# A fused attention and feed-forward kernel: wider transposes and score matmuls at the opening, two moved steps, one store on another queue

## Chip, cores and metric

The kernel runs on one core of a Trainium2 chip. The metric is the device time of one execution in microseconds (us); a kernel is given as the median of several executions. The engines are TensorE (PE; its weight loads are listed apart as PEld), VectorE (DVE), ScalarE (ACT), GpSimd (POOL) and SyncE (SP). POOL, SP and ACT also issue DMA transfers.

## What is computed

Attention with a local window of 96 positions and 8 global positions, for 4 batches, 8 heads, 768 positions and head size 64, and then a feed-forward layer from 512 to 2048 and back on its 3072 rows:

```
scores = q @ k.T / 8 + bias        # bias = -slope[head] * distance
scores = where(keep, scores, -1e9) # keep: first 8 positions, or the last 96
a = softmax(scores);  x = (a @ v), heads side by side   # 3072 x 512
r = max(x @ w_in, 0)
out = (s * r*r + b) @ w_out        # float32
```

TensorE works on bf16 copies and adds up in float32.

## The kernel before

The 3072 rows are cut into 12 granules of 256 rows (two blocks of 128), three to a batch; granule j has all 8 heads, as four head pairs `hp`. The order of the work on every engine is the order of the program text: it is written out by hand from line 856 on, and no scheduler changes it.

Per granule the steps are these.

- **Loading.** POOL issues the loads of k, q and v (L92, L104, L112), which turn float32 into bf16. All weights (`w_in` in 8 slices at L129, `w_out` in 4 at L135) go through the same POOL queue. Granule 0 alone is loaded raw by SP and ACT (L150) and cast by ACT and DVE (`cast`, L157 and L159) into `nat`, laid out as partition, head, block, element. From granule 5 on a one-element copy on POOL (`pace`, L125) holds the next loads back until some earlier result is there.
- **Transposing q and k**, so that the head's 64 elements lie on partitions (`kT`, `qT`). Granule 0: `T_mm` (L257), 8 transposes on TensorE per call, each of one head and one block (128x64). Granules 1 and 2: `T_quads` (L272), 32 transposes of 64x64 per call; their rows are spread over partitions four at a time. `T_ev` (L293) copies the result from PSUM into `kT` or `qT`, one half (two head pairs) per call, on DVE (L305) or ACT (L307). From granule 3 on SP issues DMA transposes instead (`XBk`, L319, and `XBq`, L327).
- **Scores.** `S_mm` (L406) multiplies a key block by a query block for the two heads of a pair, head 0 on the upper 64 partitions and head 1 on the lower 64. In the first granule of a batch (0, 3, 6, 9) a pair takes 6 matmuls: keys 0 with queries 0, keys 1 with queries 1, keys 0 with queries 1. In the others it takes 8. `SB_mm` (L387) adds the bias on TensorE for granule 0 and one pair of granule 1. `S_post` (L426) takes the exponential on ACT (L431); `S_mul` multiplies by a template of the bias on DVE (L441, L445). `SS` does scores and both for two pairs.
- **Attention output.** `A` (L453, matmuls at L474) and the division on DVE (L491, L492); then a transpose to `xT` on TensorE (L510, L530) or by DMA (L544).
- **First layer.** `P1(j, fp)` (L558): 8 matmuls of 128x256 (L565) for 256 of the 2048 columns, in the two `psh` PSUM buffers in turn; relu on ACT (L581, L583) or DVE; the square on DVE later (`flush` at L556, `Q` at L602).
- **Second layer.** Granules 0 to 2: `P2` (L635). From granule 3 on the product of 2x2 blocks is done with seven block products in place of eight: `W_mm` (L715, matmuls at L741), from sums of weights `W_tw` (L689, DVE, L697), made once, and sums of activations `W_sw` (L704, DVE, L713). `W_post` and `W_add` (L751) finish it, and SP stores it. `W_end` (L800) does this for the last granule with four stores: L820, L823 and twice L838.

PSUM tiles come from five pools by tag: `psh` (two buffers), `pso`, `av`, `scA` and `scB` (one each).

Two places of the hand-written order matter below. The first is at lines 932 to 948, after granule 1's attention: squares of granule 0, then `P1(0, 5)`, `P1(1, 0)` to `P1(1, 3)`, `P1(0, 6)`, and the transposes of granule 2 among the last groups. The second is lines 1077 to 1086:

```
    P1(3, 5)
    W_tw(4, 0, 4)
    P1(3, 6)
    P1(3, 7)
    flush()
    W_sw(3, 3)
    W_tw(4, 4, 8)
```

Of the kernel before, what the change touches and what calls it, by code (L numbers as in the profile page):

```python
# [9 lines left out]
BF16 = mybir.dt.bfloat16  # L10
# [8 lines left out]
def kernel(  # L19
# [13 lines left out]
    nc = tc.nc  # L33
    P = nc.NUM_PARTITIONS

    B, H, S, D = q.shape
# [4 lines left out]
    GB = 2  # L41
    GT = GB * P
# [14 lines left out]
    ldp = ctx.enter_context(tc.tile_pool(name="ldp", bufs=3))  # L57
# [81 lines left out]

    raw32 = gpool.tile([P, 2, H, GB * D], F32, name="raw32", tag="gT")  # L140
    for nm in "kq":
        nat[nm, 0] = ldp.tile([P, H, GB * D], BF16, name=f"{nm}nat", tag=f"{nm}nat")

    def first(nm, half):
        src = (q if nm == "q" else k)[0, 4 * half : 4 * half + 4, 0:GT, :]
# [6 lines left out]

    def cast(nm, half, eng=None):
        hs = slice(4 * half, 4 * half + 4)
        i, o = raw32[:, "kq".index(nm), hs, :], nat[nm, 0][:, hs, :]
        if eng is None:
            nc.vector.tensor_copy(o, i)  # L157
        else:
            nc.scalar.copy(o, i)  # L159
# [95 lines left out]
    tps = {}  # L255

    def T_mm(j, half, nm, tag="psh", own=False):  # L257
        a = 0 if nm == "k" else 1
        if own or (j, half) not in tps:
            tps[j, half] = PS[tag].tile([P, 2, 2, GT], BF16, name="ps_t", tag=tag)  # L260
        ps = tps[j, half]
        tps[j, half, nm] = ps
        for e in range(2):
            for i in range(GB):
                for hi in range(2):
                    nc.tensor.transpose(
                        ps[hi * D : (hi + 1) * D, a, e, i * P : (i + 1) * P],
                        nat[nm, j][:, 4 * half + 2 * e + hi, i * D : (i + 1) * D],
                        ident[:],
                    )  # L270

    def T_quads(j, nm, tags=("psh", "psh"), own=False, both=None):  # L272
        a = 0 if nm == "k" else 1
        if both:
            t = PS[both].tile([P, 2, 2, 2, GT], BF16, name="ps_t2", tag=both)
            for half in range(2):
                tps[j, half] = t[:, half]
        for half in range(2):
            if own or (j, half) not in tps:
                tps[j, half] = PS[tags[half]].tile([P, 2, 2, GT], BF16, name="ps_t", tag=tags[half])  # L280
            tps[j, half, nm] = tps[j, half]
        for e in range(2):
            for i in range(4):
                for half in range(2):
                    r = slice(half * D, (half + 1) * D)
                    for hi in range(2):
                        nc.tensor.transpose(
                            tps[j, half][hi * D : (hi + 1) * D, a, e, i * D : (i + 1) * D],
                            nat[nm, j][r, 2 * e + hi, i * D : (i + 1) * D],
                            ident[r, r],  # L290
                        )

    def T_ev(j, half, nm, eng=None, es=(0, 1)):  # L293
        b, g = bg(j)
        a = 0 if nm == "k" else 1
        if j not in qT:
            qT[j] = qtp.tile([P, HP, GT], BF16, name="qT", tag="qT")
        e0, e1 = es[0], es[-1] + 1
        n = GB if j == 0 else 4
        src = tps[j, half, nm][:, a, e0:e1, :].rearrange("p e (i t) -> p e t i", i=n)  # L300
        hs = slice(2 * half + e0, 2 * half + e1)
        dst = kT[b % 2][:, hs, g * GT : (g + 1) * GT] if nm == "k" else qT[j][:, hs, :]
        dst = dst.rearrange("p e (t i) -> p e t i", i=n)
        if eng is None:
            nc.vector.tensor_copy(dst, src)  # L305
        else:
            nc.scalar.copy(dst, src)  # L307
# [98 lines left out]
    def S_mm(j, hp, biased=False, which=None):  # L406
        b, g = bg(j)
        ps = sps[j, hp] if biased else sc_tile(j, hp, which)
        own = [(kT[b % 2][:, hp, (g * GB + i) * P : (g * GB + i + 1) * P], i) for i in range(GB)]
        if g == 0:  # L410
            plan = [own[0] + (0,), own[1] + (1,), (own[0][0], 1, 2)]
        else:
            ko = kos[j]
            plan = [own[0] + (0,), own[1] + (2,), (ko[:, hp, 0, :], 0, 1), (ko[:, hp, 1, :], 1, 3)]
        for n_, (kt, i, oc) in enumerate(plan):
            for hi in range(2):
                r = slice(hi * D, (hi + 1) * D)
                nc.tensor.matmul(  # L418
                    ps[:, hi, oc * P : (oc + 1) * P],
                    lhsT=kt[r, :],  # L420
                    rhs=qT[j][r, hp, i * P : (i + 1) * P],
                    start=not biased,
                    stop=not biased or n_ == len(plan) - 1,
                )
# [133 lines left out]
    def P1(j, fp, sq="dve", tag="psh", relu="act"):  # L558
        if j not in gT:
            gT[j] = gpool.tile([P, FC, GT], BF16, name="gT", tag="gT")  # L560
        ps = PS[tag].tile([P, 2, GT], F32, name="ps_1", tag=tag)
        for i in range(2):
            fc = 2 * fp + i
            for kc in range(KC):
                nc.tensor.matmul(  # L565
                    ps[:, i, :],
                    lhsT=w_in_bf[:, kc, fc * P : (fc + 1) * P],
                    rhs=xT[j][:, kc, :],
                    start=(kc == 0),
                    stop=(kc == KC - 1),  # L570
                )
# [228 lines left out]
    def W_end(j):  # L800
        o = wt.setdefault((j, "o"), work.tile([P, 2, DM], F32, name="o_pr", tag="o_pr", bufs=3))
        lo, hi = slice(0, HC), slice(HC, DM)
        W_mm(j, 1)
        W_sw(j, 2)
        W_post(j, 1)
        W_mm(j, 5)
        v = W_part(j, "u3")
        W_add(j, v, "b", bvec[:, hi])
        W_sw(j, 4)
        W_mm(j, 6)  # L810
        W_post(j, 6)
        t = W_part(j, "t")
        W_add(j, t, "b", wt[j, "u2"])
        W_mm(j, 2)
        W_post(j, 2)
        W_mm(j, 7)
        W_add(j, o[:, 1, hi], "a", v)
        u4 = W_part(j, "u1")
        W_add(j, u4, "a", bvec[:, lo])
        nc.sync.dma_start(W_rows(j)[:, 1, hi], o[:, 1, hi])  # L820
        W_mm(j, 0)
        W_add(j, o[:, 0, hi], "d", t)
        nc.sync.dma_start(W_rows(j)[:, 0, :], o[:, 0, :])  # L823
        for e in range(2):
            ps = ps_h.tile([P, 2, GT], F32, name="ps_e", tag="psh")[:, 0, 0:P]
            cs = slice(e * P, (e + 1) * P)
            for f in range(HF):
                nc.tensor.matmul(
                    ps,
                    lhsT=g_blk(j, 1, 1)[:, f, :],  # L830
                    rhs=tw[:, 3, f, cs],
                    start=f == 0,
                    stop=f == HF - 1,
                )
            nc.vector.scalar_tensor_tensor(
                out=o[:, 1, cs], in0=ps, scalar=s_bc[:], in1=u4[:, cs], op0=ALU.mult, op1=ALU.add
            )
            nc.sync.dma_start(W_rows(j)[:, 1, cs], o[:, 1, cs])  # L838
# [54 lines left out]
    A(0, 3, "pso")  # L893
    XT_half(0, 0, "act", "av")
    KO_own(0)
    T_quads(1, "q", both="scB")
    T_ev(1, 0, "q", "act")
    SB_mm(1, 0)
    XT_half(0, 1, "dve", "psh")
# [31 lines left out]
    XT_half(1, 1, "dve", "pso")  # L931
    for f in range(5):
        Q(0, f)
    P1(0, 5)
    P1(1, 0)
    P1(1, 1)
    P1(1, 2)
    P1(1, 3)
    P1(0, 6)
    T_quads(2, "k", ("pso", "av"))  # L940
    T_ev(2, 0, "k")
    T_ev(2, 1, "k", "act")
    P1(0, 7)
    T_quads(2, "q", ("pso", "av"))
    T_ev(2, 0, "q")
    T_ev(2, 1, "q", "act")
    make_tmpl(0, 2, 1, 3)
# [130 lines left out]
    Q(3, 2)  # L1078
    P1(3, 4)
    P1(3, 5)  # L1080
    W_tw(4, 0, 4)
    P1(3, 6)
    P1(3, 7)
    flush()
    W_sw(3, 3)
    W_tw(4, 4, 8)

    def P1s(j, fp, n):
# [163 lines left out]
```

## Time and profile before

| what | value |
|---|---|
| median of 5 executions | 208.61 us (208.28 to 210.1) |
| the profiled execution: its own time | 208.28 us |
| its span, first to last instruction | 206.4 us |
| PE busy | 198.6 us (96%) |
| weight loads busy | 160.4 us (78%) |
| DVE busy | 173.6 us (84%) |
| ACT busy | 114.3 us (55%) |
| POOL busy | 77.0 us (37%) |
| granted TensorE clock, mean | 0.999 |
| the chain that ended last | PE 72%, DMA 18%, POOL 6% |

The profile is one execution. Its timeline gives for a group of like instructions the start, the time from the first start to the last end, engine, line, operation, tiles, shape, count, and in brackets the idle time of the engine before it with what ended it. Matmuls are pipelined: a single 128x256 matmul of the first layer is listed with 273 ns, but eight in a row start every 0.109 us. So the price of a block of matmuls is read from its start to the start of the next block, not from the sum of its durations. The chain that ended last is followed back from the last instruction, at each step to what released it; time on that chain is what sets the end. Time of an engine off the chain can grow as long as it stays covered.

### The profile page before, as it was taken

To read this page: it belongs to the slowest core of one execution; us is meant where nothing else is said; L and a number is where in the kernel's file an instruction comes from. 1 tells how busy PE (TensorE), PEld (TensorE's weight loads), DVE (VectorE), ACT (ScalarE), POOL (GpSimd) and SP (SyncE) were. 2 spreads that over 40 slices of the span, in tenths; PEclk is the share of its full clock that TensorE was granted. 3 is DMA by queue.
4 is the path that set the end of the run, shared out by engine and by line. 5 is a ranking of instruction groups with operands and counts; after the bars stand their busy time and mean duration, and the time that the engine had idled before them with its cause. 6 is when DMAs were issued, how large, how long until landed. Compare 5 with 4: busy or idle time off the path is not lost.

```text
span 206.4 us, 5617 instructions
## 1 busy us (share of the span) xinstructions
PE 198.6 (96%) x2288; PEld 160.4 (78%) x2293; DVE 173.6 (84%) x418; ACT 114.3 (55%) x171; POOL 77.0 (37%) x98
## 2 busy tenths in 40 slices
PE   7988899999899999999999999999999999999993
PEld 2657776545765788888988988988988988988883
DVE  5887677699898999988799799788799799787693
ACT  5888588353895676636536536536446546524400
POOL 8994673854646019519029109109000000000000
PEclk9999999999999999999999999999999999999999
DMA  5999999999999988969999939999996041040022
GB/s 165 192 184 197 191 195 190 174 148 152 111 118 184 198 233 90 142 130 112 191 117 127 203 59 118 201 126 97 189 120 174 8 118 37 0 152 5 0 105 102
DMA packets 104858, 27.64 MB, mean 134 GB/s; under 512 B 91520, under 2 KB 102144, under 8 KB 104832
## 3 DMA queue, kind: packets, MB, share of 16 engines
q0 software_dynamic: 70976, 13.11, 91.9%
q1 hardware_dynamic: 32800, 13.64, 33.6%
q10 hardware_dynamic: 1056, 0.52, 0.9%
q8 instruction: 18, 0.29, 0.6%
q14 instruction: 8, 0.07, 0.2%
HBM read 27.26 MB, written 6.29 MB: 163 GB/s over the span
## 4 chain that ended last, share of the span: by engine, by line
PE 72%; DMA 18%; POOL 6%; ACT 1%; issue 1%; DVE 0%; POOLq 0%; ACTq 0%
PE ps L565 34%; PE ps_w L741 15%; PE ps_wb L741 7%; DMA w_in_bf<-in_moe_w_in_dram 5%; DMA qnat<-in_q_dram 5%; DMA w_out_bf<-in_moe_w_out_dram 4%; PE ps_wa L741 4%; PE ps_av L474 4%; PE ps_s L418 4%; DMA qT<-qnat 4%; PE ps L635 3%; POOL w_in_bf L129 2%; POOL vaug L112 2%; ACT gT L583 1%; POOL knat L92 1%
## 5 line engine op out<-in xcount | busy, mean ns | idle before, releaser
L565 PE MATMUL ps<-xT,w_in_bf 128*128 128x256 bf16 x768 | 96.2, 273 | 1.9 <-DMA w_in_bf<-in_moe_w_in_dram 1.8
L565 PEld LDWEIGHTS <-w_in_bf 128*128 128x128 bf16 x768 | 72.6, 98 | 12.4 <-DMA w_in_bf<-in_moe_w_in_dram 2.5
L583 ACT ACTIVATE gT<-ps 128x512 bf16<-128x512 f32 x72 | 43.1, 598 | 58.7 <-PE ps L565 56.5
L431 ACT ACTIVATE pt<-ps_s 128x1024 bf16<-128x1024 f32 (+1 forms) x48 | 43.1, 951 | 6.9 <-PE ps_s L418 4.6
L741 PEld LDWEIGHTS <-sw 128*128 128x128 bf16 x288 | 28.1, 98 | 3.5
L602 DVE TENSOR_TENSOR gT<-gT 128x512 bf16<-128x512 bf16 x74 | 28.1, 415 | 1.7 <-ACT gT L583 1.6
L125 POOL COPY pdum<-xT 1x1 bf16<-1x1 bf16 x5 | 6.7, 1339 | 46.0 <-DMA xT<-xn 46.0
L445 DVE TENSOR_TENSOR pt<-pt,tmpl 128x1024 bf16<-128x1024 bf16 x31 | 20.8, 685 | 2.8 <-ACT pt L431 2.8
L112 POOL DMA_DIRECT2D vaug<-in_v_dram x24 | 21.6, 919 | 4.2 <-DMA w_out_bf<-in_moe_w_out_dram 1.6
L741 PEld LDWEIGHTS <-gT 128*128 128x128 bf16 x208 | 19.7, 98 | 3.2 <-issue 0.2
L492 DVE TENSOR_TENSOR xn<-ps_av,rc 128x256 bf16<-128x256 f32 x48 | 20.4, 424 | 1.7
L635 PE MATMUL ps<-w_out_bf,gT 128*128 128x512 bf16 x76 | 18.7, 380 | 0.2
L741 PE MATMUL ps_w<-tw,sw 128*128 128x256 bf16 x144 | 18.7, 273 | 0.0
L581 ACT ACTIVATE gT<-ps 128x512 bf16<-128x512 f32 x23 | 13.6, 599 | 7.5 <-PE ps L565 7.3
L751 DVE SCALAR_TENSOR_TENSOR u<-ps_w,s_bc,bvec 128x256 f32<-128x256 f32 x27 | 12.9, 478 | 5.7 <-PE ps_w L741 5.7
L474 PEld LDWEIGHTS <-pt 128*128 128x128 bf16 x352 | 15.2, 98 | 3.1 <-DVE pt L445 0.8
L104 POOL DMA_DIRECT2D knat<-in_k_dram x18 | 15.8, 886 | 3.9 <-DMA kT<-knat 2.7
L104 POOL DMA_DIRECT2D qnat<-in_q_dram x18 | 16.0, 901 | 3.5 <-DMA w_out_bf<-in_moe_w_out_dram 2.6
L474 PE MATMUL ps_av<-vaug,pt 128*128 128x65 bf16 x224 | 16.1, 194 | 0.1
L635 PEld LDWEIGHTS <-gT 128*128 128x128 bf16 x96 | 8.7, 97 | 8.9
L418 PE MATMUL ps_s<-qT,kT 64*128 64x128 bf16 x224 | 12.7, 219 | 1.1 <-DMA qT<-qnat 1.0
L491 DVE RECIPROCAL rc<-ps_av 128x4 f32<-128x4 f32 x48 | 8.5, 177 | 5.9 <-PE ps_av L474 5.7
(102 smaller groups left out, 241.5 us busy)
## 6 DMA issues: line engine op xcount, KB each, us to landing
out_dram<-o_pr SPq DMA_DIRECT2D x19, 256.0 KB, 4.5
vaug<-in_v_dram POOLq DMA_DIRECT2D x24, 128.0 KB, 7.6
knat<-in_k_dram POOLq DMA_DIRECT2D x22, 128.0 KB, 6.0
qnat<-in_q_dram POOLq DMA_DIRECT2D x22, 128.0 KB, 7.0
w_in_bf<-in_moe_w_in_dram POOLq DMA_DIRECT2D x8, 256.0 KB, 8.2
w_out_bf<-in_moe_w_out_dram POOLq DMA_DIRECT2D x4, 512.0 KB, 10.0
out_dram<-o_pr SPq DMA_DIRECT2D x2, 512.0 KB, 2.7
raw<-in_q_dram ACTq DMA_DIRECT2D x2, 256.0 KB, 4.8
```

The source lines that it names most:

```text
L104: nc.gpsimd.dma_start(t[:, i, :, :], src[b, :, sb * P : (sb + 1) * P, :].rearrange("h p d -> p h d"))
L112: nc.gpsimd.dma_start(vaug[b % 2][:, sb, :, 0:D], v[b, :, sb * P : (sb + 1) * P, :].rearrange("h p d -> p h d"),)
L418: nc.tensor.matmul(ps[:, hi, oc * P : (oc + 1) * P], lhsT=kt[r, :], rhs=qT[j][r, hp, i * P : (i + 1) * P], start=not biased, stop=not bias ...
L431: nc.scalar.activation(pt[:, :, 0:n], ps[:, :, 0:n], ACT.Exp, scale=QSCALE)
L445: nc.vector.tensor_tensor(x, x, m.unsqueeze(2).to_broadcast((P, 2, GB, 2 * P)), ALU.mult)
L474: nc.tensor.matmul(av[:, i, hi, :], lhsT=pt[:, hi, c * P : (c + 1) * P], rhs=vv, start=n_ == 0, stop=n_ == len(ops) - 1,)
L492: nc.vector.tensor_tensor(xn[j][:, :, 2 * hp : 2 * hp + 2, :], av[:, :, :, 0:D], rc[:].to_broadcast((P, GB, 2, D)), ALU.mult,)
L565: nc.tensor.matmul(ps[:, i, :], lhsT=w_in_bf[:, kc, fc * P : (fc + 1) * P], rhs=xT[j][:, kc, :], start=(kc == 0), stop=(kc == KC - 1),)
L583: nc.scalar.activation(gs.rearrange("p f (r t) -> p f r t", r=2), ps[:].rearrange("p f (t r) -> p f r t", r=2), ACT.Relu,)
L602: nc.vector.tensor_tensor(gs, gs, gs, ALU.mult)
L635: nc.tensor.matmul(po[j, tb], lhsT=gT[j][:, fc, tb * P : (tb + 1) * P], rhs=w_out_bf[:, fc, :], start=(fc == 0), stop=(fc == FC - 1),)
L741: nc.tensor.matmul(wt[j, ps], lhsT=lhs[:, f, :], rhs=rhs[:, f, :], start=first and f == 0, stop=f == HF - 1, skip_group_check=True,)
```

## The change

Six edits:

1. Granule 0's `nat` is laid out as partition, block, head, element, and the casts write into it in that order. `T_mm` then transposes two heads at once: 4 transposes of 128x128 per call in place of 8 of 128x64.
2. `T_quads` takes all 128 partitions at once: 16 transposes of 128x64 per call in place of 32 of 64x64. Both halves of k, or of q, lie in one PSUM tile; before, a half's k and q shared a tile. Granule 1's k uses one `psh` buffer, its q `scB`; granule 2's k uses `pso`, its q `av`.
3. `S_mm` for the first granule of a batch multiplies keys 0 with both query blocks in one matmul of 256 columns, written to two separate column ranges: 4 matmuls per head pair in place of 6.
4. `P1(1, 0)` goes before `P1(0, 5)`.
5. `W_tw(4, 0, 4)` goes from before `P1(3, 6)` to after `W_sw(3, 3)`.
6. In `W_end` the store of rows 0 (L823) is issued by ACT's queue, no longer by SP's.

In all 112 matmuls and as many weight loads fewer are issued: 16 by `T_mm`, 64 by `T_quads`, 32 by `S_mm`.

```diff
-        nat[nm, 0] = ldp.tile([P, H, GB * D], BF16, name=f"{nm}nat", tag=f"{nm}nat")
+        nat[nm, 0] = ldp.tile([P, GB, H, D], BF16, name=f"{nm}nat", tag=f"{nm}nat")
...
-        i, o = raw32[:, "kq".index(nm), hs, :], nat[nm, 0][:, hs, :]
+        i = raw32[:, "kq".index(nm), hs, :].rearrange("p h (i d) -> p h i d", i=GB)
+        o = nat[nm, 0][:, :, hs, :].rearrange("p i h d -> p h i d")
...
-        tps[j, half, nm] = ps
+        tps[j, half, nm] = ps[:, a]
         for e in range(2):
+            h = 4 * half + 2 * e
             for i in range(GB):
+                nc.tensor.transpose(
+                    ps[:, a, e, i * P : (i + 1) * P],
+                    nat[nm, j][:, i, h : h + 2, :],
+                    ident[:],
+                )
+
+    def T_quads(j, nm, tag="psh"):
+        t = PS[tag].tile([P, 2, 2, GT], BF16, name="ps_t", tag=tag)
+        for half in range(2):
+            tps[j, half, nm] = t[:, half]
+        for e in range(2):
+            for i in range(4):
                 for hi in range(2):
                     nc.tensor.transpose(
-                        ps[hi * D : (hi + 1) * D, a, e, i * P : (i + 1) * P],
-                        nat[nm, j][:, 4 * half + 2 * e + hi, i * D : (i + 1) * D],
+                        t[hi * D : (hi + 1) * D, :, e, i * D : (i + 1) * D],
+                        nat[nm, j][:, 2 * e + hi, i * D : (i + 1) * D],
                         ident[:],
                     )
...
-            plan = [own[0] + (0,), own[1] + (1,), (own[0][0], 1, 2)]
+            plan = [(own[0], slice(0, GT), None), (own[1], qs[1], 1)]
...
+                if oc is None:
+                    dst = ps[:, hi].rearrange("p (a c) -> p a c", a=GB)[:, :, 0:P]
+                else:
+                    dst = ps[:, hi, oc * P : (oc + 1) * P]
                 nc.tensor.matmul(
-                    ps[:, hi, oc * P : (oc + 1) * P],
+                    dst,
                     lhsT=kt[r, :],
-                    rhs=qT[j][r, hp, i * P : (i + 1) * P],
+                    rhs=qT[j][r, hp, qc],
...
-        nc.sync.dma_start(W_rows(j)[:, 0, :], o[:, 0, :])
+        nc.scalar.dma_start(W_rows(j)[:, 0, :], o[:, 0, :])
...
-    T_quads(1, "q", both="scB")
+    T_quads(1, "q", "scB")
...
+    P1(1, 0)
     P1(0, 5)
-    P1(1, 0)
...
-    T_quads(2, "k", ("pso", "av"))
+    T_quads(2, "k", "pso")
...
-    T_quads(2, "q", ("pso", "av"))
+    T_quads(2, "q", "av")
...
-    W_tw(4, 0, 4)
     P1(3, 6)
     P1(3, 7)
     flush()
     W_sw(3, 3)
+    W_tw(4, 0, 4)
     W_tw(4, 4, 8)
```

More of the change, by code (lines that the diff above doesn't have):

```diff
@@ L261, in T_mm @@
         ps = tps[j, half]
-        tps[j, half, nm] = ps
+        tps[j, half, nm] = ps[:, a]
         for e in range(2):
+            h = 4 * half + 2 * e
             for i in range(GB):
+                nc.tensor.transpose(
[9 more added lines that the diff above has]
+            for i in range(4):
                 for hi in range(2):
                     nc.tensor.transpose(
-                        ps[hi * D : (hi + 1) * D, a, e, i * P : (i + 1) * P],
-                        nat[nm, j][:, 4 * half + 2 * e + hi, i * D : (i + 1) * D],
+                        t[hi * D : (hi + 1) * D, :, e, i * D : (i + 1) * D],
+                        nat[nm, j][:, 2 * e + hi, i * D : (i + 1) * D],
                         ident[:],
                     )
[L272 to L291, printed above, removed]
     def T_ev(j, half, nm, eng=None, es=(0, 1)):
@@ L299, in T_ev @@
         n = GB if j == 0 else 4
-        src = tps[j, half, nm][:, a, e0:e1, :].rearrange("p e (i t) -> p e t i", i=n)
+        src = tps[j, half, nm][:, e0:e1, :].rearrange("p e (i t) -> p e t i", i=n)
         hs = slice(2 * half + e0, 2 * half + e1)
@@ L408, in S_mm @@
         ps = sps[j, hp] if biased else sc_tile(j, hp, which)
-        own = [(kT[b % 2][:, hp, (g * GB + i) * P : (g * GB + i + 1) * P], i) for i in range(GB)]
+        own = [kT[b % 2][:, hp, (g * GB + i) * P : (g * GB + i + 1) * P] for i in range(GB)]
+        qs = [slice(i * P, (i + 1) * P) for i in range(GB)]
         if g == 0:
-            plan = [own[0] + (0,), own[1] + (1,), (own[0][0], 1, 2)]
+            plan = [(own[0], slice(0, GT), None), (own[1], qs[1], 1)]
         else:
             ko = kos[j]
-            plan = [own[0] + (0,), own[1] + (2,), (ko[:, hp, 0, :], 0, 1), (ko[:, hp, 1, :], 1, 3)]
-        for n_, (kt, i, oc) in enumerate(plan):
+            plan = [(own[0], qs[0], 0), (own[1], qs[1], 2)]
+            plan += [(ko[:, hp, i, :], qs[i], 2 * i + 1) for i in range(GB)]
+        for n_, (kt, qc, oc) in enumerate(plan):
             for hi in range(2):
                 r = slice(hi * D, (hi + 1) * D)
+                if oc is None:
+                    dst = ps[:, hi].rearrange("p (a c) -> p a c", a=GB)[:, :, 0:P]
+                else:
+                    dst = ps[:, hi, oc * P : (oc + 1) * P]
                 nc.tensor.matmul(
-                    ps[:, hi, oc * P : (oc + 1) * P],
+                    dst,
                     lhsT=kt[r, :],
-                    rhs=qT[j][r, hp, i * P : (i + 1) * P],
+                    rhs=qT[j][r, hp, qc],
                     start=not biased,
```

## The prediction

> **What bounds the kernel now.** I read four views, in this order. First the time by stretches (columns: stretch, its length, then busy time and instructions of PE, weight loads, DVE, ACT, POOL, and last the granted clock, DMA share and GB/s):
>
> ```profile
> 0.00:13.70 13.70, 11.93 (x187) 6.33 (x187) 10.22 (x36) 10.30 (x16) 12.95 (x24) 1.00 1.36 179
> 13.70:27.00 13.30, 11.95 (x143) 10.30 (x144) 9.65 (x25) 9.12 (x15) 8.03 (x13) 1.00 1.56 191
> 27.00:52.16 25.16, 23.98 (x260) 14.60 (x260) 21.21 (x37) 14.44 (x22) 14.81 (x19) 1.00 1.87 172
> 79.00:203.30 124.30, 124.10 (x1410) 109.36 (x1407) 107.88 (x267) 59.98 (x91) 30.29 (x35) 1.00 0.96 109
> ```
>
> From 79 to 203.3 us TensorE is busy 124.10 of 124.30 us: there, time can only come from work taken off PE. Before 52.16 it has gaps. What fills them is in the chain that ended last (start, length, what):
>
> ```profile
> 13.73 10.63 DMA w_in_bf<-in_moe_w_in_dram
> 24.37 0.28 issue
> 24.65 9.07 DMA w_out_bf<-in_moe_w_out_dram
> 33.72 0.28 issue
> 34.00 10.41 DMA qnat<-in_q_dram
> 44.43 7.68 DMA qT<-qnat
> 52.16 0.46 PE ps_s L418 x10
> ```
>
> From 13.73 to 52.16 the chain holds no compute engine: weights, then q of granule 3, then its two DMA transposes. Their issues wait only for earlier transfers (and, for k and q of granule 3, for the casts and transposes of granule 0, done by 7.7 us). Third, the timeline around that point:
>
> ```profile
> 27.26 0.45 PE L287 MATMUL ps_t<-ident,knat 64*64 64x64 bf16 x32
> 27.64 1.05 PE L565 MATMUL ps<-xT,w_in_bf 128*128 128x256 bf16 x8
> ...
> 50.92 0.23 PE L418 MATMUL ps_s<-qT,kT 64*128 64x128 bf16 x2
> 52.16 0.46 PE L418 MATMUL ps_s<-qT,kT 64*128 64x128 bf16 x10 [1.00 <-DMA qT<-qnat]
> 52.55 1.05 PE L565 MATMUL ps<-xT,w_in_bf 128*128 128x256 bf16 x8
> ```
>
> TensorE gets to the scores of granule 3 at 50.92, runs the two matmuls that need only the first half of qT, and waits for the second half. So whatever this change does to PE before 50.92, gain or loss, is held at 52.16, as long as PE comes no later than 52.16 − 50.92 = **1.24 us** after its present time. Fourth, SyncE's queue at the end:
>
> ```profile
> 202.88 0.33 SPq L823 DMA_DIRECT2D out_dram<-o_pr  x1
> 203.31 0.89 SPq L838 DMA_DIRECT2D out_dram<-o_pr  x2
> ```
>
> **T_mm and casts (granule 0, 4.4 to 7.7 us).** Each call goes from 8 transposes of 128x64 to 4 of 128x128. Eight took 0.28 to 0.34 us to the next instruction's start (5.09 to 5.37, 5.37 to 5.71, 6.91 to 7.24). Four of 128x128 (L530) took 0.22 (19.91 to 20.13). Gain 0.06 to 0.12 each, about 0.35 us for the four calls. The casts write in runs of 64 instead of 128 elements; they take 0.42 to 0.46 us on DVE and 0.60 on ACT. No row shows the new order; I bound it by nothing and by the DVE copy of 128x512 that scatters its output (L305, 0.69), so 0 to +0.27 each, two in a row on the path, and take 0. All this ends in PE's wait of 0.62 us for the first slice of w_in (13.86): zero on the end, and a loss of 0.54 would be covered too.
>
> **T_quads (granules 1 and 2).** 32 transposes of 64x64 become 16 of 128x64, whose outputs are 64x128. The old 32 take 0.38 us (27.26 to 27.64, likewise 28.62 to 29.00), 12 ns each: four run side by side. The new kind is T_mm's old row: 35 to 42 ns each, so 16 take 0.56 to 0.68, **a loss of 0.18 to 0.30 us per call**. From outside, 16 at the 55 ns of an L530 transpose would be 0.88, a loss of 0.50; the other bound is 16 at 12 ns, a gain of 0.19. I take +0.24, since the shape is T_mm's own. [...]
>
> The two calls for granule 1 (9.63, 11.12) are covered by the w_in waits at 13.86 and 16.08 (0.62 each). The two for granule 2 put PE 0.48 us late of the 1.24.
>
> **A new wait.** Both halves of a granule's k (or q) now lie in one PSUM tile, and the instruction order shows that ACT's copy of half 1 (L307) waits for DVE's copy of half 0 (L305) for granule 2. Before, they ran together:
>
> ```profile
> 27.76 0.69 DVE L305 COPY kT<-ps_t 128x512 bf16<-128x512 bf16 x1 [0.20 <-PE ps_t L287]
> 27.86 0.58 ACT L307 COPY kT<-ps_t 128x512 bf16<-128x512 bf16 x1
> ```
>
> ACT's copies of k and q start about 0.65 us later each. Behind them on ACT are the relus of P1(0,7), P1(1,4), P1(1,5), a template and the exps of granule 2; PE waits for these relus through the two psh buffers. Followed instruction by instruction, the exps go from 31.45 to about 32.3, the relu of P1(1,6) from 33.25 to about 34.1; PE, itself 0.48 late, wants that buffer for the second P2 tile at about 34.6 and may stall 0.15 us. ACT's idle 1.53 us before the exps at 36.83 swallows the rest. PE late at 50.92: 0.48 + 0.15 = 0.63 us, under 1.24. Granule 5's loads are paced by ACT at 46.58 but start at 49.45, behind another transfer: 2.5 us of cover. Cost: **0**.
>
> **P1(1,0) before P1(0,5).** P1(0,5) starts at 21.92, after 0.53 us of waiting for w_in. P1(1,0) needs the copy of xT, which runs from 21.43 to 21.85. It starts at about 21.88, P1(0,5) follows 0.87 later, and both have run by the same moment: gain 0.04, between 0 and 0.53 if the copy were earlier, and under the same cover. Relus (0.60) and squares (0.42) swap places on ACT and DVE; the P2 that needs them comes at 33.
>
> **Scores.** For granules 0, 3, 6 and 9 each head pair loses two of six matmuls; two of the remaining four are 256 wide. Sixteen matmuls of 128 columns come in groups of four 0.115 us apart (36.46, 36.57, 36.68), so a pair on the two row halves costs 57 ns; around a block lie some 0.10 us more. [...] Granule 3's first block now waits for all of qT: after 52.16 it takes 2 x (111 + 57) + 100 = 0.44 us where five pairs took 0.39: **+0.05**. The other ten head pairs of granules 3, 6 and 9 save 4 ns each, and in four of them (97.44, and its like in granule 9) ACT's relu ends the wait, not PE: **−0.03**.
>
> **W_tw(4,0,4) later.** 0.60 us of DVE moves behind three squares and sw3, which come 0.60 earlier; both W_tw end at about 79.5 as before. PE's gap there (77.9 to 78.14) ends with ACT's exp (77.07 + 1.03), not with a square: 0, at best −0.2.
>
> **Last store.** The store at 202.88 leaves SP's queue. SP issued the last two at 203.31 and 203.78, 0.47 apart, while DVE was done at 203.17 and 203.61. The two stores before them follow DVE by 0.03 us (201.98 to 202.01, 202.85 to 202.88), so they can go at 203.20 and 203.67: **−0.11**, or nothing if the gap was the wake-up; I take −0.10. ACT is idle then; its issue takes about 0.55 us (two took 1.11 at the start), and the landing of 2.0 us ends near 205.4, before the last one.
>
> **Sum**: 0 + 0.05 − 0.03 + 0 − 0.10 = −0.08 us on the profiled execution's 208.28, that is 208.2. That execution is the lowest of five; their median is 208.61, so the median forecast is **208.5 us**.
>
> **Rivals.**
> 1. *The cover runs out.* If the new transposes cost 55 ns (+0.50 per call) and ACT's delay stalls PE by 0.6 us instead of 0.15, PE is 1.6 late at 50.92 and exceeds 1.24: slower by about 0.4, less the end's 0.1, near 208.9. For it: the new wait. Against it: ACT's idle time. It decides from 1.24 us of lateness. Chance 0.12.
> 2. *256-wide score pairs do not overlap* (slower). Place: the PE-bound stretch. Price: 0.10 us on each of twelve head pairs, less 0.05 where ACT hides some, plus the 0.05 already counted: +1.1, near 209.6. It decides from about 120 ns per pair. Against it: 128-wide pairs overlap nearly fully. Chance 0.08.
> 3. *The wait at 52.16 shrinks by itself* (faster). If the q transposes land sooner in the changed kernel, at most 1.24 − 0.63 = 0.6 us is to be had, with the end 0.7: near 207.9. Nothing of the change touches these transfers. Chance 0.07.
> 4. Forecast: no difference to be seen. Chance 0.73.
>
> **Numbers.** About 0.5% (1.04 us) is what measuring this kernel can tell from no change. Rivals 1 and 3 and the forecast lie within it for their greater part, rival 2 beyond. Faster 0.06, same 0.84, slower 0.10. The range goes from 207.8 (rival 3 taken in) to 209.2 (rival 1 taken in with the 0.3 by which single times spread); rival 2 is left out.
>
> **What would show it.** Right: 16 transposes of granule 2 in 0.56 to 0.68 us, ACT's copies behind DVE's, PE's wait before granule 3's scores down from 1.24 to 0.5 to 0.8 us, the first L565 after it at about 52.6, blocks of granules 6 and 9 shorter by under 0.03, last issue near 203.67. Wrong: no wait left at granule 3, score blocks of 0.5 us and more, or a chain that leaves the DMA before 52.

## The result, and the profile after

The changed kernel takes 210.94 us in the median of 30 executions (208.82 to 213.8), the kernel before 208.85 in 51 (207.58 to 212.72). The ratio is **1.0062, 95% interval 1.0036 to 1.0087**: slower by about 1.3 us, and outside the predicted range. The medians lie 2.1 us apart, more than the ratio says, because 18 of the 31 executions after whose clock is on record ran at a mean granted clock under 0.995, against 40 of the 119 of the kernel before that stand beside the experiments, and the ratio leaves the slowest executions out. The profiled execution took 209.54 us (before 208.28), its span 207.8 us (before 206.4), at a mean granted clock of 1.000: the same 1.3 us.

The chain of waits of the changed kernel, from the weights to granule 3's scores (start, length, what):

```profile
13.74 10.60 DMA w_in_bf<-in_moe_w_in_dram
...
24.62 9.06 DMA w_out_bf<-in_moe_w_out_dram
...
33.97 10.65 DMA qnat<-in_q_dram
...
44.63 8.68 DMA qT<-qnat
...
53.45 0.51 PE ps_s L417 x8
```

The chain goes through the same transfers as before. The loads of q take 0.24 us more, and q's two DMA transposes 1.00 more: the scores start at 53.45, where they started at 52.16. From that start to the end it is 154.35 us, before 154.24. So the whole loss lies ahead of granule 3's scores. TensorE's timeline there (start, length, what, idle time before it and what ended it):

```profile
50.31 1.03 PE L634 MATMUL ps<-w_out_bf,gT 128*128 128x512 bf16 x4
53.45 0.51 PE L417 MATMUL ps_s<-qT,kT 64*128 64x256 bf16 x8 [2.11 <-DMA qT<-qnat]
53.88 1.05 PE L564 MATMUL ps<-xT,w_in_bf 128*128 128x256 bf16 x8
```

TensorE arrives at 51.3, some 0.4 us later than before, well inside the 1.24. Its wait did not shrink, it grew, from 1.24 (1.00 of it listed, behind the two matmuls that ran first) to 2.11: the transfer came later than TensorE did.

What happened to the transfer stands in the DMA view. Of the changed kernel from 49 to 53 us, the bandwidth in 40 slices of 0.1 us, and the line of queue q8 (packets, MB, share). I read q8 as the queue of TensorE's instructions, from its count (below) and because its packets come earlier when idle matmuls are added (the one at 39.3 us before comes at 37.1 with 16 of them, b_fill16w):

```profile
GB/s 150 159 146 144 146 145 146 310 116 128 140 141 136 152 152 151 137 74 42 23 10 12 5 8 10 8 9 10 10 8 44 137 133 233 150 145 147 150 151 197
q8 instruction: 1, 0.02, 2.2%
```

One packet of 16 KB goes out at 49.8 us (the slice of 310; 16 KB in 0.1 us is 164 GB/s on top of the 146 beside it). About 0.9 us later, from 50.7 to 52.0, the core's whole DMA traffic falls from 150 to some 10 GB/s (5 to 12 from 51.0 on), while q's transposes are in flight. The kernel before, in the same window and then from 57 to 61:

```profile
GB/s 105 126 110 108 104 152 129 150 156 145 115 188 211 173 173 158 149 145 160 151 141 155 119 149 143 136 146 148 172 157 161 250 95 50 47 38 28 31 24 31
```
```profile
GB/s 154 151 155 310 119 138 166 166 164 154 140 152 129 29 0 0 0 4 6 8 8 12 8 10 9 13 115 147 142 149 156 160 164 154 161 156 150 143 155 154
q8 instruction: 1, 0.02, 2.2%
```

It has the same standstill, with the same burst ahead of it, but at 58.3 to 59.5, after granule 3's scores have begun. In the first of the two windows its traffic falls too, from 52.2 on, as q's transposes have landed: less far, to 24 to 50 GB/s from 52.3 on, and with no fetch of TensorE ahead of it. So there are falls of another origin beside the standstill. Its fetches lie at 39.3 and 57.4 us, those of the changed kernel at 34.8, 49.8 and 63.9. The page counts 18 such fetches before and 17 after (0.29 and 0.28 MB, 16 KB each), for 4581 and 4357 listed TensorE instructions (matmuls and weight loads): one per about 254 before (4581/18) and per about 256 after (4357/17).

The steps that the prediction did work out, in the timeline of granule 2's transposes:

```profile
27.12 0.64 PE L280 MATMUL ps_t<-ident,knat 128*64 128x128 bf16 x16
...
27.69 1.05 PE L564 MATMUL ps<-xT,w_in_bf 128*128 128x256 bf16 x8
27.80 0.69 DVE L298 COPY kT<-ps_t 128x512 bf16<-128x512 bf16 x1 [0.39 <-PE ps_t L280]
...
28.53 0.58 ACT L300 COPY kT<-ps_t 128x512 bf16<-128x512 bf16 x1 [0.70 <-DVE kT L298]
```

Sixteen transposes take 0.57 us to the next matmul, and ACT's copy stands behind DVE's. And at the end:

```profile
204.17 0.80 DVE L834 SCALAR_TENSOR_TENSOR o_pr<-ps_e,s_bc,u 128x128 f32<-128x128 f32 x2
204.24 0.37 ACTq L822 DMA_DIRECT2D out_dram<-o_pr  x1
204.55 0.84 SPq L837 DMA_DIRECT2D out_dram<-o_pr  x2
```

### The profile page after: what moved, and what is told of

Read it like the earlier page. It is cut to its first block, busy times and chain, and to the rows that moved or that the text cites. A ratio compares the mean times of both kernels' runs of the same rounds, so it can differ in the third digit from the quotient of the medians.

```text
span 207.8 us, 5396 instructions
## 1 busy us (share of the span) xinstructions
PE 199.1 (96%) x2176; PEld 160.1 (77%) x2181; DVE 173.9 (84%) x418; ACT 114.4 (55%) x171; POOL 76.8 (37%) x98
## 4 chain that ended last, share of the span: by engine, by line
PE 71%; DMA 19%; POOL 6%; ACT 1%; issue 1%; DVE 0%; POOLq 0%; ACTq 0%
PE ps L564 33%; PE ps_w L740 15%; PE ps_wb L740 7%; DMA qnat<-in_q_dram 5%; DMA w_in_bf<-in_moe_w_in_dram 5%; DMA w_out_bf<-in_moe_w_out_dram 4%; DMA qT<-qnat 4%; PE ps_wa L740 4%; PE ps_s L417 4%; PE ps_av L473 4%; PE ps L634 3%; POOL w_in_bf L129 2%; POOL vaug L112 2%; ACT gT L582 1%; POOL knat L92 1%
## 5 line engine op out<-in xcount | busy, mean ns | idle before, releaser
L740 PEld LDWEIGHTS <-gT 128*128 128x128 bf16 x208 | 19.7, 98 | 3.3 <-issue 0.6
L417 PE MATMUL ps_s<-qT,kT 64*128 64x128 bf16 (+1 forms) x192 | 12.6, 228 | 2.2 <-DMA qT<-qnat 2.1
```

Of the source, the lines that this page charges most:

```text
L417: nc.tensor.matmul(dst, lhsT=kt[r, :], rhs=qT[j][r, hp, qc], start=not biased, stop=not biased or n_ == len(plan) - 1,)
L740: nc.tensor.matmul(wt[j, ps], lhsT=lhs[:, f, :], rhs=rhs[:, f, :], start=first and f == 0, stop=f == HF - 1, skip_group_check=True,)
```

## The theories

- **A.** The change takes 112 matmuls and their weight loads off TensorE, most of them early. That moves its instruction fetches, one per about 254 to 256 listed instructions, later in time. One that falls among granule 3's DMA transposes stops the transfers for about 1.2 us.
- **B.** The edits' own work (slower `T_quads`, copies one behind the other, TensorE late) costs the time.
- **C.** Granule 5's loads start while q's transposes are in flight and take bandwidth from them.

A "fill" is an idle matmul on constants, most of them of 32 (or 16) columns, in the warm-up ahead of the first transposes, where TensorE waits for data; it counts as two instructions, a matmul and a weight load, and computes nothing that is used. The warm-up before has 9 of 512 columns; a net number is told.

All runs, with the fetch of q8 between 35 and 52 us, the start of granule 3's scores that need all of qT, and TensorE's wait ahead of them in the profile:

| kernel | fetch, us | scores, us | wait, us | ratio (95%) |
|---|---|---|---|---|
| before | 39.3 | 52.16 | 1.00 | 1 |
| after | 49.8 | 53.45 | 2.11 | 1.0062 (1.0036 to 1.0087) |
| after_late5 | 50.0 | 53.49 | 2.27 | 1.011 (1.0049 to 1.0171) |
| after_fill88 | 39.2 | 53.69 | 1.18 | 1.004 (1.0005 to 1.0075) |
| before_fill80 | 46.4 | 52.61 | none | 1.0047 (1.0023 to 1.0072) |
| before_fill40 | 50.4 | 52.98 | 1.38 | 1.0079 (1.0045 to 1.0112) |
| b_quads | 45.1 | 56.06 | 0.86 + 3.64 | 1.0191 (1.0131 to 1.025) |
| b_quads_fill64 | 38.4 | 52.99 | 1.39 | 0.9994 (0.9957 to 1.0032) |
| b_fill40w | 49.1 | 53.49 | 2.43 | 1.0062 (1.0021 to 1.0103) |
| b_fill72w | 44.3 | 53.15 | 0.45 + 1.44 | 1.0055 (1.0012 to 1.0098) |
| b_fill16w | 37.1 | 52.43 | 1.55 | 1.0007 (0.9976 to 1.0038) |
| a_fill40w | 45.8 | 53.13 | 1.07 | 1.0089 (1.0048 to 1.013) |
| a_fill88w | 41.9 | 54.69 | none | 1.014 (1.0065 to 1.0215) |
| a_noquads_fill24w | 39.6 | 52.82 | 1.53 | 1.0105 (1.0039 to 1.0172) |
| a_noquads_fill44w | 35.3 | 51.67 | 0.50, for ACT | 0.9966 (0.9928 to 1.0004) |
| a_fill74w | 40.3 | 53.67 | 1.93 | 1.0012 (0.997 to 1.0055) |
| a_fill78m | 40.6 | 51.83 | none | 1.006 (1.0017 to 1.0102) |
| a_fill82m | 40.4 | 52.91 | 0.69 | one execution |
| a_fill76m | 40.6 | 52.60 | 0.58 | one execution |

Over all 19 profiles two things can be counted. First, each has one fetch between 44 and 61 us. In 17 of them the traffic falls to a mean of 7 to 30 GB/s, 0.8 to 2.0 us after that fetch, mostly for 0.5 to 1.4 us. The exceptions are before_fill80 and before_fill40. Second, where q's transposes stand on the chain, it gives their time to landing: 8.47 to 10.14 us in the six profiles with the fetch at 45 to 50.4 us (after, after_late5, before_fill40, b_quads, b_fill40w, a_fill40w), 7.75 in b_fill72w with the fetch at 44.3, and 7.25 to 7.71 in six with a fetch at 37 to 41 (before, b_quads_fill64, b_fill16w, a_noquads_fill24w, a_fill82m, a_fill76m). But it is 8.32 in after_fill88 and 8.76 in a_fill74w, whose fetches lie at 39.2 and 40.3. In these two and in before_fill40 the shallower fall comes before q has landed, at 52.2 to 52.8 us; what sets it off is open.

## The experiments

**Theory C: granule 5's loads later.** The changed kernel, with the loads held until granule 3's exponential.

```diff
-    pace(raw[1, 0][0:1, 0:1])
-    load_granule(5)
...
     SS(3, (0, 1))
+    pace(pts[3, 0][0:1, 0, 0:1])
+    load_granule(5)
```

> The changed kernel, with granule 5's loads held back until the first exponential of granule 3 is done (about 54 us in place of 48.7). Theory C: without these loads beside them the q transposes land at least 1 us earlier and the time is 0.5% or more below the changed kernel's, about that of before. Theory A: the fetch at 49.8 us and its standstill stay; only what the loads themselves take from the transposes in 48.7 to 52 us comes back, 0 to 0.5 us, so 1.003 to 1.007 of before. Theory B: 1.006, no change.

The fetch stayed at 50.0 us and the standstill at 51.0 to 52.0, the scores started at 53.49, the ratio was 1.011. C falls.

**First fills.** The changed kernel with 88 more, which is what the change takes away ahead of granule 3, and the kernel before with 80 and 40. Part of them stand in the first layer (`P1`), ahead of its matmuls:

```diff
-    idle(9, "av")
+    idle(7, "av")
+    idle(30, "av", 16)
...
+        for _ in range(FILL.get((j, fp), 0)):
+            nc.tensor.matmul(ps[:, 0, 0:16], ...)
```

> The changed kernel, with 88 more tiny matmuls (16 columns of constants, results overwritten) where TensorE waits anyway: in the warm-up and ahead of four first-layer groups before 23 us. They put back the 176 TensorE instructions that the change took out before 50 us. Theory A (the 16 KB fetches of TensorE's instructions moved: one now falls at 49.8 us, among the DMA transposes of granule 3's q, and all transfers stand still from about 50.9 to 52.1): the fetch goes back to about 39 us, the scores of granule 3 start near 52.2 and the time returns to that of before, 0.998 to 1.002 of it. Theory B (the cost is the change's own transposes, copies and waits on TensorE and ScalarE): nothing returns, 1.005 to 1.010 of before. Theory C (granule 5's loads, issued 0.7 us earlier in the changed kernel, press on the q transposes): nothing returns either.

> The kernel before, unchanged but for 80 tiny matmuls in the same waiting places, 160 instructions. Theory A: the fetch that lay at 57.4 us comes at about 49.4 us, transfers stand still before the q transposes of granule 3 have landed, the wait ahead of granule 3's scores grows from 1.0 to about 2.2 us, and the time becomes 1.004 to 1.009 of before. Theories B and C: the same time as before, 0.998 to 1.002, since none of the change's edits is in it.

> The control: the kernel before with 40 tiny matmuls, 80 instructions. All theories expect the time of before, 0.998 to 1.002, since the filling lies in waits. By theory A the fetches go from 39 and 57 to about 36 and 54.5 us, both outside of the q transposes of granule 3 (data between 42 and 51 us). If this one is slower than before, the filling itself costs something and the first two kernels say less.

With 88 the fetch went back to 39.2 us, and the median to 208.81 (before, on the same chip, 208.79), though the ratio is still 1.004. The 60 fills in the first layer took about 25 ns each (18 of them 0.46 us, from 14.95 to 15.41), 1.5 us in all, and TensorE came to granule 3 only at 52.5, so this run mixes two things. With 80 on the kernel before TensorE itself was late (no wait was left), so it does not test A. With 40 it was meant as a control with its fetch at 54.5; the fetch came at 50.4, and the kernel was slower by 0.8%: not the control that it was to be. It looks like a hint for A, but the DMA view of this run from 49 to 53 us speaks against the standstill as the only cause:

```profile
GB/s 169 154 154 144 147 160 160 167 161 145 201 196 223 384 169 149 136 145 136 152 133 146 117 136 132 141 146 168 166 188 188 210 78 63 60 55 50 49 61 55
```

After the fetch (the slice of 384) the traffic stays at 117 GB/s or more up to 52.1, and q landed at 52.9 all the same. From here on fills stand in the warm-up alone, except in the last group.

**T_quads alone, and with its count restored.** The kernel before with the edit of `T_quads` only (64 matmuls, 128 instructions fewer), and the same with net 64 fills:

```diff
+                for hi in range(2):
+                    nc.tensor.transpose(
+                        t[hi * D : (hi + 1) * D, :, e, i * D : (i + 1) * D],
+                        nat[nm, j][:, 2 * e + hi, i * D : (i + 1) * D],
...
-    idle(9, "av")
+    idle(3, "av")
+    idle(70, "av", 32)
```

The part below the dots is in the second kernel only.

> The kernel before with the change's T_quads alone: 16 transposes per call, one PSUM tile, no other edit; 128 TensorE instructions fewer before 30 us. Theory A (the moved fetch): the fetch that lay at 39 us comes 128 instructions later, at about 49 to 50 us, into the q transposes of granule 3; the scores of granule 3 start at 53 us or later, and the time is 1.004 to 1.009 of before. Theory B (own cost of the transposes and copies): TensorE is up to 0.6 us later at 51 us, under the wait, and the time is 0.999 to 1.003 of before.

> The same, with 64 more tiny matmuls (32 columns of constants), all in the warm-up ahead of 4.8 us, six wide warm-up matmuls replaced by 70 small ones; this restores the count of TensorE instructions, 128 of them. Theory A: the fetches are back at about 39 and 57 us and the time is that of before, 0.998 to 1.002. Theory B: the same time as the kernel with T_quads alone, whatever that is.

The edit alone costs **1.9%** (1.0191), three times the whole change. The same edit with its instructions given back as idle matmuls costs **nothing** (0.9994). The transposes, the copies one behind the other and TensorE's lateness are the same in both; what differs is the count and with it where the fetches fall, the one ahead of granule 3 at 45.1 or 38.4 us. B falls for `T_quads`, within the interval of 0.4% either way. q's transposes on the two chains, the edit alone first:

```profile
45.88 10.14 DMA qT<-qnat
```
```profile
45.58 7.37 DMA qT<-qnat
```

So 2.8 of the 3.1 us between the two starts of the scores (56.06 and 52.99) lie in these transposes. The standstill after the fetch at 45.1 lasts only from 47.0 to 47.8, so it does not explain all of the 2.8; the traffic falls again at 52.6 to 53.0, with no fetch of TensorE near, and why is open. TensorE's timeline of the first, and the row of the second:

```profile
52.19 0.23 PE L410 MATMUL ps_s<-qT,kT 64*128 64x128 bf16 x2 [0.86 <-DMA qT<-qnat]
56.06 0.72 PE L410 MATMUL ps_s<-qT,kT 64*128 64x128 bf16 x10 [3.64 <-DMA qT<-qnat]
56.71 1.89 PE L557 MATMUL ps<-xT,w_in_bf 128*128 128x256 bf16 x8
```
```profile
52.99 0.46 PE L410 MATMUL ps_s<-qT,kT 64*128 64x128 bf16 x10 [1.39 <-DMA qT<-qnat]
```

The first shows a second price. After a wait of 3.64 us eight first-layer matmuls take 1.89 us, not 1.05, and the ten score matmuls 0.72, not 0.46: TensorE's granted clock has dropped. The time by stretches (the number after POOL's is the clock) has 0.87 for it from 52 to 79 us, and 1.00 with the fills:

```profile
52.00:79.00 27.00, 23.07 (x235) 16.02 (x238) 18.71 (x43) 15.85 (x24) 10.36 (x13) 0.87 1.81 147
```
```profile
52.00:79.00 27.00, 25.84 (x287) 19.09 (x289) 24.36 (x58) 19.59 (x30) 10.08 (x11) 1.00 1.98 164
```

**Fills alone on the kernel before.** Net 40 (shown), 72 (2 of 512 columns and 79 of 32) and 16 (7 and 18) in the warm-up, nothing else changed:

```diff
-    idle(9, "av")
+    idle(5, "av")
+    idle(44, "av", 32)
```

> The kernel before with 40 more tiny matmuls (80 instructions), now all in the warm-up, so that TensorE comes to no later step later than before. In the run with as many instructions added, part of them after 13 us, the second fetch lay at 50.4 us. Theory A: it lies there again (49 to 51 us) and the time is 1.003 to 1.008 of before. Theory B: 0.998 to 1.002.

> The kernel before with 72 more tiny matmuls (144 instructions), all in the warm-up. Theory A: the second fetch comes at about 46 to 48 us, early in the q transposes; in the run with 160 instructions it lay at 46.4 us and no standstill followed, so the time should be near that of before again, 0.998 to 1.003, although more was added than in the kernel with 40. Theory B: 0.998 to 1.002. If filling as such costs time, this one is slower than the one with 40.

> The kernel before with net 16 tiny idle matmuls in the warm-up, a control for the fills. Theory A: the fetch moves from 39.3 to about 37 us and the one after from 57.4 to about 56, both away from the transposes: ratio 0.998 to 1.002, scores of granule 3 at 52 to 53 us. If idle matmuls in the warm-up cost by themselves (as 40 and 72 of them did): 1.002 to 1.006.

Idle work alone, ahead of everything, makes the kernel 0.6% slower when the fetch falls at 49.1 us and changes nothing when it falls at 37.1; 64 fills with `T_quads` (fetch at 38.4) had cost nothing either. So it is not the fills that cost. With 72 A's expectation was wrong: I had expected the fetch at 46 to 48 us and no harm from it, as the run with 80 fills had its fetch at 46.4 and seemed to show no standstill (its traffic does fall to 9 GB/s, but for 0.3 us alone, at 49.8). The fetch came at 44.3, and the transposes' packets run from about 42.5 us on; the traffic stood at 5 to 23 GB/s from 46.2 to 47.0 and the scores came at 53.15. The dangerous stretch is wider than I had put it: every kernel with a fetch at 44 to 50.4 us was slower, by 0.5 to 1.9%.

**Fills on the whole change, in the warm-up.** Net 40 (5 of 512 columns and 44 of 32) and net 88 (1 and 96).

> The changed kernel with net 40 tiny idle matmuls more in the warm-up. Theory A: 80 instructions move the fetch from 49.8 to about 44 to 45 us, still among the transposes: a standstill of the transfers about 0.9 us after it, scores of granule 3 after 53.0, ratio 1.004 to 1.02 (the upper end if the clock drops after a wait of more than 2.4 us). If idle matmuls in the warm-up help by themselves, in proportion to their number: about half of what 88 bring, ratio 1.001 to 1.004. Theory B: as the changed kernel, 1.004 to 1.009.

> The changed kernel with net 88 tiny idle matmuls more in the warm-up alone, so that TensorE's instruction count ahead of granule 3 is that of the kernel before. Theory A (a 16 KB instruction fetch of TensorE that falls among granule 3's DMA transposes stops the transfers): the fetch moves from 49.8 to about 39 us and the next to about 58 to 59, the scores of granule 3 start at 52.0 to 53.0 with a wait of 0.7 to 1.6 us, clock 1.00 in 52 to 79 us, ratio 0.997 to 1.002. Theory B (the edits' own work on TensorE and the chained copies cost the time): scores at about 53.4 as in the changed kernel, ratio 1.004 to 1.009. If it is faster than 0.997, the end store and the smaller scores bring what the prediction gave them.

Forty moved the fetch to 45.8, still among the transposes, and brought nothing (1.0089): idle matmuls do not help in proportion to their number. Eighty-eight missed, 1.014. The first fetch now fell at 6.6 us, among the loads of granule 1; these landed 6.8 to 6.9 us after their issue (before 4.7 to 4.9), TensorE waited for them, and its granted clock fell to 0.66 in 10 to 14 us and 0.50 in 14 to 18. It tells nothing of granule 3.

**All edits but T_quads.** `T_quads` as before, the other five edits kept, net 24 fills (shown; it restores the count ahead of granule 3), and then net 44 (5 and 48):

```diff
-    T_quads(2, "k", "pso")
+    T_quads(2, "k", ("pso", "av"))
...
-    idle(9, "av")
+    idle(6, "av")
+    idle(27, "av", 32)
```

> The changed kernel with the edit of T_quads taken back (32 transposes of 64x64 in two tiles, as before), all other edits kept, and net 24 tiny idle matmuls in the warm-up, which restore the instruction count ahead of granule 3. Theory A: fetch at about 39 us, ratio 0.997 to 1.001, since the only edits left are those that save or move little. Theory B with T_quads as the culprit gives the same, 0.997 to 1.001; with any of the other edits as the culprit, 1.003 to 1.009.

> The changed kernel with the edit of T_quads taken back and net 44 (not 24) tiny idle matmuls in the warm-up: 40 instructions more than the run with 24, whose profile had an instruction fetch of TensorE at 205.5 us, among the last stores, and a tail 1.5 us longer than elsewhere. Theory A: the fetch ahead of granule 3 at about 37 to 38 us, the last one at 200 to 202 us and none among the last stores; the stretch from the first L835 result to the end 3.5 to 3.7 us instead of 5.1; ratio 0.997 to 1.002. If one of the five edits that are left costs time by itself: again 1.004 to 1.011, with the profile showing a place other than a fetch.

With 24 the scores came at 52.82, as A has it, yet the kernel was slower (1.0105). The profile shows the place at the other end: the stretch from the first `L835` result to the end (line L842 there) is 5.1 us, where every other profile has 3.5 to 3.7. The DMA view from 205 to 209 us:

```profile
GB/s 307 277 267 297 251 435 93 0 0 0 0 0 0 0 10 5 10 10 10 10 10 15 0 0 0 0 0 0 0 0 0 0 0 0 0 0 0 0 0 0
q8 instruction: 1, 0.02, 1.4%
```

A fetch at 205.5 us (the slice of 435), in the middle of the last stores, nothing for 0.7 us, and the last few packets at 206.4 to 207.2. Twenty fills more are 40 instructions more: the last fetch is then at 200.0, the traffic of the last stores runs through, and the kernel is at **0.9966 (0.9928 to 1.0004)**. The DMA view of that run from 203 to 207 us:

```profile
GB/s 0 0 0 246 389 451 369 369 369 333 282 297 262 272 246 52 0 0 0 0 0 0 0 0 0 0 0 0 0 0 0 0 0 0 0 0 0 0 0 0
```

So the five edits without `T_quads` cost nothing, and the pair differs by 20 idle matmuls.

**The whole change with its fetch out of the way.** Net 74 in the warm-up (1 and 82); or net 64 there and 7 (shown), 6 or 9 of 16 columns ahead of each of `P1(0, 0)` and `P1(0, 1)`: 78, 76, 82.

```diff
-    idle(9, "av")
+    idle(3, "av")
+    idle(70, "av", 32)
...
+    FILL = {(0, 0): 7, (0, 1): 7}
```

> The whole changed kernel with net 74 tiny idle matmuls in the warm-up, 14 fewer than the run with 88, whose first fetch fell at 6.6 us among the loads of granule 1 and made them land 2 us later. Theory A: first fetch at 8 to 9 us and no late granule 1 loads, clock 1.00 throughout, the fetch ahead of granule 3 at 40 to 42 us, scores of granule 3 at 52.0 to 53.2 us, no fetch among the last stores; ratio 0.998 to 1.003. Theory B (the edits' own work on TensorE and the chained copies): 1.004 to 1.009 as the changed kernel, scores at about 53.4 with a fetch that is out of the way.

> The whole changed kernel with net 64 tiny idle matmuls in the warm-up, as in the run of T_quads alone with its count restored, and 7 more ahead of each of P1(0,0) and P1(0,1), where TensorE waits for w_in. Theory A: first fetch at 8 to 11 us, the fetch ahead of granule 3 at 40 to 41 us, scores of granule 3 at 52.0 to 53.2 us at a clock of 1.00, none among the last stores, ratio 0.997 to 1.003. Theory B: scores at about 53.4 although no fetch falls among the transposes, ratio 1.004 to 1.009.

> One look at the kernel with net 78 fills with four fills more ahead of the first layer (8 instructions). That kernel's times fell into two groups at one clock, 208.2 to 209.1 and 210.65 to 211.0 us; its profile, of the first group, had no fetch among the last stores. Theory A with a second place: if this execution is near 208.6, no fetch of TensorE after 201 us and 3.5 to 3.7 us from the first result of the last product to the end; if it is near 210.6, a fetch at 203.5 to 206 us and 5 to 5.7 us there. If it is near 210.6 without such a fetch, the second group has another cause.

> The same look with two fills fewer than 78 (4 instructions). Either near 208.6 us without a fetch of TensorE after 201 us, or near 210.6 with one at 203.5 to 206 us and a tail of 5 to 5.7 us; granule 3's scores at 51.5 to 53.2 us in both cases. Near 210.6 without a late fetch: another cause.

The fetch went to 40.3 to 40.6 as expected. In three profiles the scores start at 51.83, 52.91 and 52.60, not at 53.45: there, with the change in place, the loss at granule 3 is gone or partly gone. In the fourth, with 74 fills, they start at 53.67 after a wait of 1.93 us, later than in the changed kernel, although its fetch lies at 40.3; A does not explain it. The ratios are 1.0012 (74) and 1.006 (78). The second misses A's expectation; of the 13 executions with 74 fills six took 212.1 to 213.3 us at a mean clock of 0.992. All three profiles, and that of 74 fills, show a new wait, which no other profile has, here of the kernel with 78:

```profile
122.87 1.05 PE L750 MATMUL ps_w<-w_out_bf,gT 128*128 128x256 bf16 x8
124.39 0.81 PE L574 MATMUL ps<-xT,w_in_bf 128*128 128x256 bf16 x6 [0.47 <-DMA xT<-xn]
```

A first-layer group waits 0.3 to 0.5 us for `xT`, which comes by DMA transposes issued at 118.7 to 121.2 (78 fills); a fetch falls at 121.4. Times of this kernel fall into two groups at one clock, 208.2 to 209.1 (5) and 210.65 to 211.0 (6), beside one at 212.57 at a lower clock. The kernels with 82 and 76 fills, one execution each, were to show the second group in a trace; they took 209.81 and 209.18 us, without a late fetch, and did not show it. What makes the second group is **not settled**.

## Why the prediction was wrong

- **The bound** was read rightly: the loss lies in the chain's DMA stretch, and from granule 3's scores on nothing changed (154.35 us against 154.24).
- **The step that failed** is "whatever this change does to PE before 50.92, gain or loss, is held at 52.16", with its twin in rival 3, "Nothing of the change touches these transfers". I took the waits for data and queues as the only ties between TensorE and the transfers. A third was in the profile of before and I did not read it: the page lists the queue of TensorE's instructions beside those of the transfers, as a share of the same 16 DMA engines (q8: 18 packets, 0.29 MB, 0.6%). Taking 88 matmuls and their weight loads off ahead of granule 3 moved a fetch from 39.3 to 49.8 us, and the transposes landed about 1.2 us later. For `T_quads`, the part with the most instructions, the count is shown to be the cause: the edit alone +1.9%, with the instructions given back −0.1%. That it acts through the fetch is read from the traces, where the standstill follows it. For the whole change the trace shows the standstill while q is in flight, and q landing late by as much; but of its five profiles with the fetch moved to 39 to 41 us three lose the delay or part of it and two (74 fills, and 88 in two places) do not. So the fetch is one cause there and not the only one, and that no rest of B is left is not shown, since none of its versions with fills came out below the kernel before.
- **`T_mm`, `T_quads`.** `T_mm`'s four transposes took 0.24 us from 5.37 to the next matmul (forecast 0.22), the casts 0.42 to 0.60 as before. `T_quads`: forecast 0.56 to 0.68 us for sixteen, measured 0.57 twice.
- **The new wait** is there (0.70 and 0.5 us of ACT's idle time, DVE's copy ends it). TensorE late by 0.63 was forecast, 0.4 measured: covered, as I had it. Rival 1 did not come.
- **Scores.** 0.43 us for granule 3's block (forecast 0.44), and 0.57 for granule 6's eight matmuls to the next block (98.77 to 99.34), where its twelve took 0.58. Rival 2 did not come. No run shows the 111 ns that the forecast takes for a pair of 256 columns: in granule 6's block one such pair takes 0.12 us to the start of the next pair (98.77 to 98.89), the other 0.11 (98.94 to 99.05).
- **`P1(1, 0)`, `W_tw`.** `P1(1, 0)` started at 22.01 (forecast 21.88), under the cover; neither shows in the time, as forecast.
- **The last store.** Forecast −0.10. SP's last stores are indeed issued earlier, 0.38 us after the last product's first result began (before 0.49); but from there to the end it is 3.63 us, before 3.58: the two stores land 2.0 us after issue, not 1.8. The 0.11 was given back in the landing. Why is open.
- **Right sign of a rival, wrong mechanism.** The slower case got 0.10, for score pairs that do not overlap; this way was not among the rivals.

## What to carry to other kernels

Before you cost an edit that adds or removes instructions ahead of a wait for a DMA, list the instruction fetches of the engine in question and shift them: here TensorE had one per about 254 to 256 listed instructions, and one among DMA transposes or last stores went with a loss of 1 to 2 us (scores 1.3 us later after, 53.45 against 52.16; a tail of 5.1 us against 3.5 to 3.7 in a_noquads_fill24w), more than the edit itself. To tell an edit's own cost from such a shift, give the instruction count back with idle matmuls where the engine waits anyway, and look at all fetches, since fills that mend one place can spoil another. In this kernel idle work alone lost a few tenths of a per cent (net 40 fills on the kernel before: 1.0062), or won more than that (20 more fills without `T_quads`: 1.0105 to 0.9966).

## What the runs showed of the hardware

- A 16 KB fetch of TensorE while DMA transposes are in flight: about 0.9 us later the core's whole DMA traffic stands nearly still for about 1.2 us (50.7 to 52.0 after, 58.3 to 59.5 before; 150 GB/s to some 10). In 17 of 19 profiles such a fall follows the fetch between 44 and 61 us, 0.8 to 2.0 us after it. Fetches of the kernel before at 13.3, 19.7 and 30.2 us, with plain loads in flight, leave no such gap (163 GB/s or more in each 0.1 us of the 2.7 us behind each).
- The fetch is not the only thing that moves q's landing: with the fetch out of the way, scores that waited for it started between 52.16 and 53.69 us.
- The clock: waits of 2.43 us (40 fills) and of 0.45 and 1.44 close together (72 fills) went with a granted clock of 0.94 in 52 to 79 us, 3.64 with 0.87; waits of 2.27 (after_late5), 2.11 (after) and 1.39 went with 1.00, one of 1.93 (74 fills) with 0.94. So the length of the wait alone does not decide.
